# P V of a windowed attention in 128x64 tiles of two heads, with the values stored beside their zeros

## The chip, the cores and the metric

One core of one Trainium2 chip runs the whole program. The time is the device time of one execution in microseconds (us); the median of several executions counts. A profile is one further execution, taken by the hardware profiler. The engines are PE (TensorE, matmuls; PEld is its weight load), DVE (VectorE), ACT (ScalarE), POOL (GpSimd) and SP (SyncE, which here only issues DMAs and small waits). Each engine works through its own list of instructions in order, and waits at semaphores for the others.

## What is computed

The inputs are bf16: x of 2048 rows and 448 columns, the weights wqkv (448 x 1344) and wo (448 x 448) of an attention with 16 heads of 28 channels, and the weights w1 (448 x 1792) and w2 (1792 x 448) with biases b1, b2 of a feed-forward part. Each position attends to itself and to the positions 2, 4, ..., 14 before it.

```python
def _A_ref(x, wqkv, wo):
    H = 16; Dh = D // H
    W, dil = 8, 2
    q, k, v = ...
    idx = pos[:, None] - (jnp.arange(W) * dil)[None, :]
    logits = jnp.einsum("bhsd,bhswd->bhsw", q, kg) * Dh ** -0.5
    attn = _softmax(jnp.where(mask, logits, -1e9), axis=-1)
    o = jnp.einsum("bhsw,bhswd->bhsd", attn, vg)
    return o.reshape(B, S, D) @ wo
def _B_ref(x, w1, b1, w2, b2):
    return _gelu(x @ w1 + b1) @ w2 + b2
xn = _layernorm(A_x)
return A_x + _A_ref(xn, ...) * _silu(_B_ref(xn, ...))
```

## The kernel before

**Rows.** The rows are regrouped, even positions first and odd positions after, so that a window of 8 positions at distance 2 becomes 8 neighbours. There are 16 row tiles of 128 rows (`t`) and 4 chunks of 512 (`c`).

**Stages.** For each row tile: statistics (L434, L439), the normed x (L469) and its transpose into `xnT`, through PE for tiles 0 to 3 (L484) and by a transposing DMA on SP for the others (L389, `turn_x`). From `xnT` PE makes q and k (L569), copied to `qk_tok` (L328 on ACT, L330 on DVE) and transposed by DMA into `qkT`; and v (L592), copied to `v_tok`, stored in DRAM (`v_hbm`, L381, `store_v`) and read back from there in windows (`move_v`, also L381). The feed-forward part is L645 (with the gelu on ACT, L649) and L677; its gate is L717, L723, L727. The output projection with `wo` is L835, L843, then L850, L856 and the store L860.

**A visit of the attention.** There are 9 visits `b` of up to 228 positions, in 4 sub-blocks `s` of 57 (`NW`; visit 4 has 56). The keys of a sub-block are 64 neighbours, 57 and the 7 before them. `spread` copies the keys into `kd` (L629 on ACT, L631 on DVE) so that two heads stand side by side: keys of one head in columns 0 to 63, of the other in 64 to 127, each with the other head's channels multiplied by zero. The scores (L744, step "S") are 32 matmuls of a 64-row, 128-column tile over 57 streamed columns: 128 partitions of the result are 64 keys of one head and 64 of the other. ACT takes the exponential (L753) into `E`, four banks a visit, and DVE multiplies by a mask (L759). Then P V (L773, step "P"): for each of 4 sub-blocks, 4 channel groups `g`, 2 pairs `h` and 2 heads of a pair `a` one matmul that contracts the 64 keys of that head and gives 32 partitions, 28 channels and a sum of the weights that comes from a column of ones beside the values. That is 64 matmuls of a 64-row, 32-column tile; head `a` goes to bank `a`. For each of the two banks DVE transposes (L782), takes the reciprocal of the sums (L786), transposes back (L791) and multiplies into `oT` (L796).

**Values.** A `v_tok` row holds 2 x 8 x 32 elements, 28 channels and 4 ones per head. `move_v` reads for each head of the pair a window of 64 rows for 4 sub-blocks, 512 bytes a run, into partitions 0 to 63 or 64 to 127 of a ring `p_v` of 3 buffers.

**Order.** The program is planned before it is emitted: every step is a task with an engine, a cost in us, dependencies and a priority (the tables `PRIO`, `LATER` and `NUDGE`); the planner fills the engines, and the instructions are emitted in that order. Rings (`_Pool`) stand for buffers. Most row pairs run as two half pairs with a hop between them: a half-array matmul group, a no-op on POOL or SP that waits for it, and the other half. A P V takes a place in `p_f`, one place, given back 3.5 us (`BURST`) after the P V. `take` and `give` name what a task occupies. In the planner a P V costs 0.52 and a score step 0.48.

Of the kernel before, what the change touches and what calls it, by code (L numbers as in the profile page):

```python
# [8 lines left out]
F32 = mybir.dt.float32  # L9
BF16 = mybir.dt.bfloat16  # L10
# [7 lines left out]
TILED = 30  # L18
BURST = 3.5
NUDGE = {  # L20
    82: 164, 83: 221, 88: -17, 98: 114, 148: -76, 155: 52, 210: 248, 309: -202, 522: -191, 633: 96,
    635: 30, 656: -230, 898: 200, 985: 15,
}
LAST = 336
SAME = 20
HOPS = ("POOL", ("SP", "POOL"))
MASK_ON = ("DVE", 0.4)

# [147 lines left out]
def kernel(  # L176
# [51 lines left out]
    def sb(name, shape, dt=BF16):  # L228
        return const.tile(shape, dt, name=name)
# [24 lines left out]
    zero = sb("zero", [P, H * 32])  # L254
    mv = sb("mv", [P, NT, 2], F32)
    sd = sb("sd", [P, NT], F32)
    rstd = sb("rstd", [P, NT], F32)
# [6 lines left out]
    p_E = ring("E", 8, [P, 512], fifo=True)  # L264
    p_dt = ring("dt", 2, [P, 512], F32)
    p_rd = ring("rd", 2, [P, H], F32)
    p_y = ring("y", 2, [P, D], F32)
    p_t = ring("t", 2, [P, D], F32)
# [14 lines left out]
    PRIO = {  # L283
        "project": (213.5, 84.5, 145, 57.5,),
        "project2": (61, 74.5, 113.5, -640,),
        "values": (199.5, -20, 128, 6,),
        "attn": (784, 1451, 452, 363, 27.5, 240.5, 361.5, 160.5, 204.5,),
        "ff1": (198.5, 215, 158, 71.5, 146.5, 194, 121, 197.5, 124, 116, 171.5, 143, 137, 144.5,
            114.5, 194, 150.5, 78.5, -21, 12, 47, 112.5, 51.5, 61.5, 93.5, 59.5, 175, 137,),
        "gelu": (5, 143.5, 52.5, 123.5,),  # L290
        "ff2": (805.5, -34.5, 231, 114.5, -2.5, 89, -623.5, 135, 208.5, 180.5, -39.5, 104, -4, 131,
            -80.5, -689,),
        "final": (-141.5, 2, -11, -16.5, 187, -2, 125, 203, -49.5, 65.5, -59.5, 162.5, -51, 134,
            6.5, 220.5,),
        "norm": (131, 11, 219.5, 294, 190, 208.5, 173, -1.5, 189, 173.5, 166.5, 159, 150.5, -11.5,
            127, 56,),
        "loads": (2.5, 106.5, -29, 61, -61,),
        "stats": (49, 32, 205.5, 205.5, 55, 91.5, -4.5, 56, 70.5, 178.5, 31, 101.5, -704, 2.5, 161,
            70.5,),
        "turn_x": (198, 4.5, 200, 12.5, 20.5, 38.5, 81, 163, 190.5, 214.5, 8.5, -3, 72, 153.5,  # L300
            72.5, 162.5,),
        "turn_qk": (-12.5, 15, 13, 198, 91, 58, -98.5, 69, 181.5, 168, 69.5, -36, 142, 100, 88,
            80.5,),
        "move_v": (19.5, -58, -99, 107.5, 62, 44, 64.5, 3, 68,),
        "store_v": (55.5, 68.5, -38.5, -16, 175.5, 53, 3.5, 13.5, 115.5, -7, 113, 144.5, 69, 170.5,
            147.5, 61.5,),
        "spread": (120, 175.5, 70.5, 58.5, 20, 222, 105.5, 24, 126,),
        "copies": (187, 4, 219, 15.5, 90, 177, 88.5, 31, 29, 20.5, 182, 51, 204.5, 49.5, 24,),
    }
    LATER = {"swap": 102.5, "qk": -548.5, "v": 174.5, "gelu": 131.5, "exp": 44, "mask": -436, "pv": 158.5, "recip": 165.5, "os": 191, "y": 231, "tanh": -35.5, "g": 111.5, "sg": 40, "o": 208.5}  # L310

    plan = _Plan()

# [272 lines left out]
    def vproj(t, prio):  # L586
        k0 = t * P

        def part(ps, kt, half, start, stop):
            r = half_rows(half)  # L590
            w = w_in[r, kt, 2 * D:] if kt < 3 else w_in3[r, 1, :]
            return nc.tensor.matmul(ps[:, :D], xnT[r, kt, k0:k0 + P], w, start=start, stop=stop)  # L592

        def evac(a, own, i):
            v = v_tok[t % len(v_tok)]

            def fn(k):
                copy(k.on, v[:, :, :, :DH].rearrange("p a x c -> p x a c"),
                     buf(p_b, own, i)[:, :D].rearrange("p (x a c) -> p x a c", a=2, c=DH))
# [163 lines left out]
    def values_of(b, exps):  # L763
        n = VIS[b][1]

        def fn(banks):
            for s in range(4):
                for g in range(G):
                    for h in range(2):
                        for a in range(2):  # L770
                            r = slice(NK * a, NK * a + NK)
                            c0, c1 = (4 * h + s) * n, (G * (s % 2) + g) * n
                            nc.tensor.matmul(banks[a][32 * g:32 * g + 32, c0:c0 + n], buf(*v_at[b])[r, s, 2 * g + h, :],  # L773
                                             buf(p_E, exps[2 * h + s // 2])[r, c1:c1 + n], start=True, stop=True)
        return fn, tuple((p_E, e, 0) for e in exps) + (v_at[b],)

    def output_of(b, po, i, a, prio):
# [28 lines left out]
    def attn(b, what):  # L806

        prio = PRIO["attn"][b]
        if what == "S":
            fn, deps, give = scores_of(b)  # L810
            a = plan.add("PE", 0.48, lambda k: fn([buf(p_b, k, i) for i in range(4)]), deps + state["early"] + last_visit[what][-1:] + last_visit["P"][b - 2:b - 1],
                         prio, take=(p_b,) * 4, give=give, tail=0.15, mode=64)
# [5 lines left out]
        a = plan.add("PE", 0.52, lambda k: fn([buf(p_b, k, i) for i in range(2)]), masked + t_v[b] + last_visit[what][-1:],  # L818
                     prio + LATER["pv"], take=(p_b, p_b, p_f), give=give, tail=0.15, mode=33)
        plan.add("CLK", 0.0, None, [a], 300, give=((p_f, a, 0),), tail=BURST)  # L820
        last_visit[what].append(a)
# [199 lines left out]
```

## Time and profile before

| | us |
|---|---|
| median of 3 runs | 153.42 (153.25 to 153.74) |
| the profiled execution | 153.43 |
| its span | 151.7 |
| granted PE clock | 1.00 |
| DMA | 19.47 MB, 36983 packets |

The span runs from the first to the last instruction; the profiled execution has 1.73 us around it. In the lists of groups each row has the line, engine, operation, what is written and read, the shape and the count, then busy time, mean duration in ns of one, and idle time before them. On a time line each row has the start in us, the time from the first start to the last end, the engine, the line, and in brackets what ended an idle time before it. Matmuls overlap, so the busy time of a group is less than count times duration.

### The profile page before, as it was taken

The numbers are of one execution on the slowest core, as the hardware profiler recorded it, in microseconds if no ns is written. First come the engines' busy times: TensorE is split into PE (matmuls) and PEld (weight loads), VectorE is DVE, ScalarE is ACT, GpSimd is POOL, SyncE is SP. The second block draws the span as 40 slices with busy tenths as digits, with TensorE's granted clock in tenths as the row PEclk, the third lists the DMA queues.
The fourth block names the chain that finished last, engine by engine and source line by source line (L and its number), as shares of the span: only waits on it lengthen the run. The fifth ranks groups of instructions, "written<-read, shape, count | busy, mean of one in ns | idle before, by whom it ended". The sixth has DMA issues, their size and how long they took to land.

```text
span 151.7 us, 5225 instructions
## 1 busy us (share of the span) xinstructions
PE 146.6 (97%) x2169; PEld 79.7 (53%) x2169; DVE 118.7 (78%) x288; ACT 90.5 (60%) x160; POOL 24.9 (16%) x62
## 2 busy tenths in 40 slices
PE   7999999999999999999999999999999999999990
PEld 2457555555567555556555554445566444554560
DVE  3786850624996997799998998889898978997972
ACT  3234969368796959658444457967396497602030
POOL 7435540100046900231201000000000000000000
PEclk9999999999999999999999999999999999999999
DMA  5999985499987973699945516222020000001221
GB/s 158 315 297 318 175 233 123 41 172 338 250 187 194 212 188 77 133 185 210 184 131 130 140 57 133 78 73 62 12 65 6 0 0 4 4 0 61 90 68 31
DMA packets 36983, 19.47 MB, mean 128 GB/s; under 512 B 24840, under 2 KB 35919, under 8 KB 36959
## 3 DMA queue, kind: packets, MB, share of 16 engines
q1 hardware_dynamic: 35774, 16.40, 47.4%
q0 software_dynamic: 1040, 2.62, 6.9%
q8 instruction: 17, 0.28, 0.7%
q10 hardware_dynamic: 144, 0.11, 0.3%
q14 instruction: 8, 0.06, 0.1%
HBM read 9.42 MB, written 3.94 MB: 88 GB/s over the span
## 4 chain that ended last, share of the span: by engine, by line
PE 95%; DVE 2%; ACT 0%; issue 0%; DVEq 0%; ACTq 0%
PE bank L645 28%; PE bank L677 25%; PE bank L569 14%; PE bank L592 7%; PE bank L835 7%; PE bank L773 4%; PE bank L699 3%; PE bank L343 3%; PE bank L744 2%; PE bank L484 1%; DVE sg L850 1%; DVE w_in L727 1%; PE bank L843 0%; DVE qk_tok L330 0%; ACT t L723 0%
## 5 line engine op out<-in xcount | busy, mean ns | idle before, releaser
L645 PE MATMUL bank<-xnT,w 64*128 64x512 bf16 x392 | 44.3, 376 | 0.0
L677 PE MATMUL bank<-w,h 64*128 64x448 bf16 x392 | 40.4, 349 | 0.0
L649 ACT ACTIVATE h<-bank,b 128x512 bf16<-128x512 f32 x56 | 34.0, 688 | 9.7 <-PE bank L645 9.3
L645 PEld LDWEIGHTS <-w 64*128 64x128 bf16 x392 | 20.4, 94 | 20.4
L677 PEld LDWEIGHTS <-h 64*128 64x128 bf16 x392 | 19.2, 94 | 16.0
L569 PE MATMUL bank<-w_in,xnT 64*128 64x448 bf16 (+1 forms) x212 | 25.1, 349 | 0.1
L753 ACT ACTIVATE E<-bank 128x456 bf16<-128x456 f32 (+1 forms) x36 | 16.8, 557 | 9.3 <-PE bank L744 9.3
L328 ACT CAST qk_tok<-bank 128x448 bf16<-128x448 f32 x23 | 11.5, 540 | 9.9 <-PE bank L569 8.5
L723 ACT ACTIVATE t<-y 128x448 f32<-128x448 f32 x15 | 8.6, 586 | 14.5 <-DVE y L717 14.5
L569 PEld LDWEIGHTS <-xnT 64*128 64x128 bf16 (+1 forms) x212 | 11.7, 94 | 9.4 <-DVE xnT L330 0.3
L782 DVE STREAM_TRANSPOSE dt<-bank 128x480 f32<-128x480 f32 (+1 forms) x18 | 12.1, 674 | 2.8 <-PE bank L773 2.8
L592 PE MATMUL bank<-w_in,xnT 64*128 64x448 bf16 (+1 forms) x106 | 13.5, 349 | 0.1
L791 DVE STREAM_TRANSPOSE dt<-rd 128x480 f32<-128x480 f32 (+1 forms) x18 | 12.1, 675 | 0.6
L835 PE MATMUL bank<-wo,oT 64*128 64x448 bf16 x112 | 12.4, 349 | 0.0
L434 DVE BATCH_NORM_STATS2 st<-x_sb 128x6 f32<-128x448 bf16 x16 | 9.6, 604 | 3.3 <-DMA x_sb<-in_A_x_dram 3.3
L759 DVE TENSOR_TENSOR E<-E,m_gen 128x456 bf16<-128x456 bf16 (+1 forms) x32 | 11.1, 387 | 1.3 <-ACT E L753 1.3
L796 DVE TENSOR_TENSOR oT<-bank,dt 128x456 bf16<-128x456 f32 (+1 forms) x18 | 11.4, 631 | 0.6
L330 DVE CAST qk_tok<-bank 128x448 bf16<-128x448 f32 x9 | 5.4, 618 | 7.8 <-ACT h L649 5.5
L717 DVE TENSOR_TENSOR y<-bank,b 128x448 f32<-128x448 f32 x15 | 8.9, 618 | 1.6 <-PE bank L677 1.6
L381 POOL DMA_DIRECT2D v_hbm<-v_tok x11 | 6.3, 572 | 21.3 <-PE bank L592 10.0
L592 PEld LDWEIGHTS <-xnT 64*128 64x128 bf16 (+1 forms) x106 | 6.0, 94 | 4.5 <-issue 0.3
L835 PEld LDWEIGHTS <-oT 64*128 64x128 bf16 x112 | 5.5, 94 | 5.1
(72 smaller groups left out, 143.7 us busy)
## 6 DMA issues: line engine op xcount, KB each, us to landing
out_dram<-o SPq DMA_DIRECT2D x15, 112.0 KB, 1.7
v<-v_hbm SPq DMA_DIRECT2D x13, 128.0 KB, 3.2
v_hbm<-v_tok POOLq DMA_DIRECT2D x11, 128.0 KB, 3.6
w<-in_B_w_dram SPq DMA_DIRECT2D x2, 672.0 KB, 7.5
x_sb<-in_A_x_dram SPq DMA_DIRECT2D x3, 448.0 KB, 6.9
w_in<-in_A_wqkv_dram SPq DMA_DIRECT2D x3, 336.0 KB, 4.4
w<-in_B_w_dram SPq DMA_DIRECT2D x2, 448.0 KB, 5.3
w<-in_B_w_dram SPq DMA_DIRECT2D x2, 336.0 KB, 6.5
```

The costliest lines, as they stand in the source:

```text
L328: nc.scalar.copy(o, i)
L569: return nc.tensor.matmul(ps[:, :D], xnT[r, kt, cs], w, start=start, stop=stop)
L592: return nc.tensor.matmul(ps[:, :D], xnT[r, kt, k0:k0 + P], w, start=start, stop=stop)
L645: return nc.tensor.matmul(ps[:], w1[r, kt, ms], xnT[r, kt, cs], start=start, stop=stop)
L649: nc.scalar.activation(buf(p_h, own, i)[:], buf(p_b, own, i)[:], ACT.Gelu_apprx_tanh, bias=b1[:, mt:mt + 1])
L677: return nc.tensor.matmul(ps[:, :D], buf(*h_at[(c, mt)])[r, cs], w2[r, mt, :], start=start, stop=stop)
L753: nc.scalar.activation(buf(p_E, k)[:, :8 * n], buf(p_b, a, at + i)[:, :8 * n], ACT.Exp, scale=SCALE)
L759: nc.vector.tensor_tensor(out=E, in0=E, in1=m[:, :, :, :n].rearrange("p i g q -> p (i g) q"), op=ALU.mult)
L782: nc.vector.transpose(buf(p_dt, k)[:, :32 * m], buf(p_b, po, i)[:, :32 * m])
L791: nc.vector.transpose(buf(p_dt, d)[:, :32 * m].rearrange("p (b c) -> p b c", c=32), buf(p_rd, r)[:, :m].unsqueeze(2).to_broadcast((P, m, 32)))
L796: nc.vector.tensor_tensor(out=oT[:, a::2, q:q + 4 * n1], in0=buf(p_b, po, i)[:, :n].rearrange("p (l q) -> p l q", l=2), in1=buf(p_dt, d)[: ...
L835: return nc.tensor.matmul(ps[:, :D], oT[r, kt, t * P:(t + 1) * P], wo[r, kt, :], start=start, stop=stop)
```

## The change

The tile shape of P V. One matmul now contracts all 128 partitions of `E`, the 64 keys of both heads of a pair, and gives 64 partitions, 32 for each head. Its weights are a 128 x 64 block: the values of the first head in rows 0 to 63 and columns 0 to 31, those of the second in rows 64 to 127 and columns 32 to 63, and zeros elsewhere. There are 32 such matmuls a visit, and the channel group `g` decides bank and half (`i = g // 2`, `r = 64 * (g % 2)`). The loop over `h` is now the outer one.

The zeros are part of the stored values. `v_tok` is 2 x 8 x 64 elements; it is set to zero and then to one in the four columns beside each head. `v_hbm` has 1024 elements a row in place of 512, `p_v` doubles, and stores and moves carry 256 KB in place of 128 KB. The 7 rows ahead of the first position come from `wo`, which is zero at that time, in place of a buffer of zeros.

Because heads now lie in other partitions of the result, `wo` is loaded in 8 DMAs of 50 KB in place of 4 of 100 KB. `xnT` and `oT` are two views of one buffer `xT` of 3072 columns: `oT` columns 1024 to 2047 lie on `xnT` columns 0 to 1023. `p_E` and `p_dt` are cut to the width in use. `p_f` has three places, and the score steps take one too. The planner's costs are 0.44 and 0.41. The tables `PRIO`, `LATER` and `NUDGE` have new values throughout, so the order on every engine is a new one.

```diff
-    xnT = sb("xnT", [P, KT, S])
+    xT = sb("xT", [P, KT, HALF + S])
+    xnT, oT = xT[:, :, HALF:], xT[:, :, :S]
-    v_tok = [sb(f"v_tok{t}", [P, 2, H // 2, 32]) for t in range(4)]
-    v_hbm = dram.tile([BACK + S, H * 32], BF16, name="v_hbm")
-    oT = sb("oT", [P, KT, S])
+    v_tok = [sb(f"v_tok{t}", [P, 2, H // 2, 64]) for t in range(NV)]
+    v_hbm = dram.tile([BACK + S, H * 64], BF16, name="v_hbm")
...
-    p_v = ring("v", 3, [P, 4, H // 2, 32], fifo=True)
+    p_v = ring("v", 3, [P, 4, H // 2, 64], fifo=True)
-    p_f = _Pool([None])
+    p_f = _Pool([None] * 3)
...
-    t_vw = [plan.add("DVE", 0.08, memset("vector", v[:, :, :, DH:], 1.0), [t_on], prio=96) for v in v_tok]
+    t_vw = []
+    for v in v_tok:
+        t_vz = plan.add("DVE", 0.42, memset("vector", v[:], 0.0), [t_on], prio=94)
+        for a in range(2):
+            t_vz = plan.add("DVE", 0.07, memset("vector", v[:, a, :, 32 * a + DH:32 * a + 32], 1.0), [t_vz], prio=94)
+        t_vw.append(t_vz)
...
-                at = v_hbm[q:q + NK, a * H * 16:(a + 1) * H * 16]
-                return bass.AP(tensor=at.tensor, offset=at.offset, ap=[list(at.ap[0]), [n * H * 32, 4], [1, H * 16]])
+                at = v_hbm[q:q + NK, a * H * 32:(a + 1) * H * 32]
+                return bass.AP(tensor=at.tensor, offset=at.offset, ap=[list(at.ap[0]), [n * H * 64, 4], [1, H * 32]])
...
-            for s in range(4):
-                for g in range(G):
-                    for h in range(2):
-                        for a in range(2):
-                            r = slice(NK * a, NK * a + NK)
-                            c0, c1 = (4 * h + s) * n, (G * (s % 2) + g) * n
-                            nc.tensor.matmul(banks[a][32 * g:32 * g + 32, c0:c0 + n], buf(*v_at[b])[r, s, 2 * g + h, :],
-                                             buf(p_E, exps[2 * h + s // 2])[r, c1:c1 + n], start=True, stop=True)
+            for h in range(2):
+                for s in range(4):
+                    for g in range(G):
+                        i, r = g // 2, 64 * (g % 2)
+                        c0, c1 = (4 * h + s) * n, (G * (s % 2) + g) * n
+                        nc.tensor.matmul(banks[i][r:r + 64, c0:c0 + n], buf(*v_at[b])[:, s, 2 * g + h, :],
+                                         buf(p_E, exps[2 * h + s // 2])[:, c1:c1 + n], start=True, stop=True)
...
-    t_zero = plan.add("DVE", 0.27, memset("vector", zero[:], 0.0), [t_on], prio=90)
-    t_vpad = dma("SP", v_hbm[:BACK, :], zero[:BACK, :], 7, 70, [t_zero, t_x[TPC - 1]])
+    t_vpad = dma("SP", v_hbm[:BACK, :], wo[:BACK].rearrange("p l d -> p (l d)")[:, :H * 64], 14, 70, [t_wo[0], t_x[TPC - 1]])
...
-    t_wo += [dma("POOL", wo[32 * g:32 * g + 28, :, :], A_wo[112 * g:112 * g + 112, :].rearrange("(l c) d -> c l d", l=4),
-                 100, 80, [t_w2[1][0]] + t_wo[:1]) for g in range(G)]
+    for k in range(8):
+        gh, r = k // 4, k % 4
+        r0 = DH * (8 * gh + 4 * (r // 2) + r % 2)
+        src = A_wo[r0:r0 + 3 * DH, :].rearrange("(l c) d -> c l d", l=3)[:, 0:3:2, :]
+        t_wo.append(dma("POOL", wo[32 * r:32 * r + DH, gh::2, :], src, 50, 80, [t_w2[1][0]] + t_wo[:1]))
```

In the new order the four moves of visits 0 and 1 stand on SP (visit 0) behind the loads of x tiles 8 to 15 and on POOL (visit 1) behind the load of b2; the transposes of qk tiles 6, 4 and 5 follow the moves on SP, and the kd copies of visit 2 stand on DVE ahead of the last mask of visit 0. The output projection of row tiles 0 and 1 stands behind the P V of visits 1 and 2.

More of the change, by code (lines that the diff above doesn't have):

```diff
@@ L25 @@
 SAME = 20
+NV = 4
 HOPS = ("POOL", ("SP", "POOL"))
@@ L253 @@
     head = sb("head", [P, 2], F32)
-    zero = sb("zero", [P, H * 32])
     mv = sb("mv", [P, NT, 2], F32)
@@ L263 @@
     p_st = ring("st", 4, [P, 6], F32)
-    p_E = ring("E", 8, [P, 512], fifo=True)
-    p_dt = ring("dt", 2, [P, 512], F32)
+    p_E = ring("E", 8, [P, 8 * NW], fifo=True)
+    p_dt = ring("dt", 2, [P, 480], F32)
     p_rd = ring("rd", 2, [P, H], F32)
@@ new lines @@
+        "project": (199, 149.5, 133, -6.5,),
+        "project2": (-22, 7, 6, -1011,),
+        "values": (133, -902.5, 8, -172.5,),
+        "attn": (120.5, 128, 32, 142, 254.5, 234.5, -63, 107.5, 74,),
+        "ff1": (56, 18.5, 198, 41, 152.5, 23, 14, 69.5, 23.5, 85, 46.5, 13.5, 60, 105.5, -94.5, 14,
+            13.5, 209.5, 178.5, 107, 155.5, 19, 94.5, 45.5, 181.5, 78, 191, 15.5,),
+        "gelu": (200, 143.5, 52.5, 60,),
+        "ff2": (39, -34.5, 118, 114.5, 188, 89, -988.5, 135, -59.5, 180.5, -25.5, 104, 52.5, 131,
+            -5, -9.5,),
@@ new lines @@
+        "final": (107, 2, -13, -16.5, 169.5, -2, 39, 203, -907, 65.5, 141, 162.5, 150.5, 134, 29,
+            125,),
+        "norm": (131, 11, 219.5, 294, 99, 106.5, 54, 161.5, 155.5, 80.5, 185, 96, 6, 122.5, 199.5,
+            50.5,),
+        "loads": (-38.5, 192.5, -18, 68.5, -61,),
+        "stats": (49, 32, 205.5, 205.5, 184.5, 160, 100, 201.5, 5, 100.5, 216.5, 20, -18.5, 57,
+            101, 180,),
+        "turn_x": (198, 4.5, 200, 12.5, 33, 125.5, 99.5, 69.5, 71.5, 137.5, 157.5, 178.5, 116,
+            157.5, -75, 19,),
@@ L308 @@
+        "turn_qk": (46.5, -8, 155, 102.5, -74, -87.5, -13.5, -50, -13.5, 168, -6, 65.5, 148, 155,
+            44.5, 20,),
+        "move_v": (185.5, -654.5, 104, 36.5, 207, 157.5, -16.5, 109.5, 194,),
+        "store_v": (147, 19.5, 134, 15.5, 59.5, 170, 47.5, 92, 166.5, 124.5, -33, 100, 170.5, 202,
+            139, 11.5,),
+        "spread": (158.5, 82.5, 155, -33.5, 71.5, 119, 127.5, 33, 131.5,),
         "copies": (187, 4, 219, 15.5, 90, 177, 88.5, 31, 29, 20.5, 182, 51, 204.5, 49.5, 24,),
@@ L309 @@
     }
-    LATER = {"swap": 102.5, "qk": -548.5, "v": 174.5, "gelu": 131.5, "exp": 44, "mask": -436, "pv": 158.5, "recip": 165.5, "os": 191, "y": 231, "tanh": -35.5, "g": 111.5, "sg": 40, "o": 208.5}
+    LATER = {"swap": 946, "qk": -94.5, "v": -72, "gelu": 216, "exp": 306.5, "mask": -1022.5, "pv": 64.5, "recip": 158.5, "os": 200, "y": 473.5, "tanh": 117.5, "g": 132, "sg": 201.5, "o": 212}
     plan = _Plan()
@@ L597, in fn @@
             def fn(k):
-                copy(k.on, v[:, :, :, :DH].rearrange("p a x c -> p x a c"),
-                     buf(p_b, own, i)[:, :D].rearrange("p (x a c) -> p x a c", a=2, c=DH))
+                at = v[:, 0, :, :DH]
+                dst = bass.AP(tensor=at.tensor, offset=at.offset, ap=[list(at.ap[0]), list(at.ap[1]), [64 * (H // 2) + 32, 2], list(at.ap[2])])
+                copy(k.on, dst, buf(p_b, own, i)[:, :D].rearrange("p (x a c) -> p x a c", a=2, c=DH))
             t_vt[t] = plan.add(("ACT", "DVE"), (act(D), dve(D)), fn, [a, t_vw[t % len(v_tok)], t_vd.get(t - len(v_tok))], prio + LATER["v"], give=((p_b, own, i),))
@@ L810, in attn @@
             fn, deps, give = scores_of(b)
-            a = plan.add("PE", 0.48, lambda k: fn([buf(p_b, k, i) for i in range(4)]), deps + state["early"] + last_visit[what][-1:] + last_visit["P"][b - 2:b - 1],
-                         prio, take=(p_b,) * 4, give=give, tail=0.15, mode=64)
+            a = plan.add("PE", 0.44, lambda k: fn([buf(p_b, k, i) for i in range(4)]), deps + state["early"] + last_visit[what][-1:] + last_visit["P"][b - 2:b - 1],
+                         prio, take=(p_b,) * 4 + (p_f,), give=give, tail=0.15, mode=64)
+            plan.add("CLK", 0.0, None, [a], 300, give=((p_f, a, 0),), tail=BURST)
             last_visit[what].append(a)
@@ L817, in attn @@
         fn, give = values_of(b, exps)
-        a = plan.add("PE", 0.52, lambda k: fn([buf(p_b, k, i) for i in range(2)]), masked + t_v[b] + last_visit[what][-1:],
+        a = plan.add("PE", 0.41, lambda k: fn([buf(p_b, k, i) for i in range(2)]), masked + t_v[b] + last_visit[what][-1:],
                      prio + LATER["pv"], take=(p_b, p_b, p_f), give=give, tail=0.15, mode=33)
```

28 lines of the change are left out of this document (2 added, 26 removed).

## Prediction

> **What bounds the kernel now.** I read four views in this order: the page's engine lines and its chain of waits, the chain in order of time, the groups by form, and stretches of the time line. The page first: PE is busy 97% of the span, and the chain is PE for 95%.
>
> ```profile
> PE 146.6 (97%) x2169; PEld 79.7 (53%) x2169; DVE 118.7 (78%) x288; ACT 90.5 (60%) x160; POOL 24.9 (16%) x62
> PE 95%; DVE 2%; ACT 0%; issue 0%; DVEq 0%; ACTq 0%
> PE bank L645 28%; PE bank L677 25%; PE bank L569 14%; PE bank L592 7%; PE bank L835 7%; PE bank L773 4%; PE bank L699 3%; PE bank L343 3%; PE bank L744 2%; PE bank L484 1%; DVE sg L850 1%; DVE w_in L727 1%; PE bank L843 0%; DVE qk_tok L330 0%; ACT t L723 0%
> ```
>
> So a microsecond taken from PE between 6.5 us (first projection) and 147 us is a microsecond of the span, and every new wait of PE is one too. The chain in order of time has one step there that is not PE: a copy on DVE.
>
> ```profile
> 42.14 0.61 DVE qk_tok L330
> 42.76 0.04 issue
> 42.80 2.80 PE bank L592 x27
> ```
>
> One of 28 L592 matmuls had started before it, so PE stood still for about 0.3 us. Everything else is gapless. The P V step is small: line L773 is 9 visits of 64 matmuls, L744 (scores) 9 visits of 32.
>
> ```profile
> L773 PE MATMUL bank<-E,v 64*32 64x57 bf16 x512 | 5.6, 189 | 0.0
> L744 PE MATMUL bank<-qkT,kd 64*128 64x57 bf16 x256 | 5.0, 186 | 0.0
> ```
>
> A matmul lasts 186 to 189 ns but they overlap, so the price of a visit is read from starts on PE's time line.
>
> ```profile
> 63.02 0.70 PE L773 MATMUL bank<-E,v 64*32 64x57 bf16 x64
> 63.65 3.58 PE L569 MATMUL bank<-w_in,xnT 64*128 64x448 bf16 x36
> ...
> 68.39 0.62 PE L744 MATMUL bank<-qkT,kd 64*128 64x57 bf16 x32
> 68.84 0.73 PE L569 MATMUL bank<-w_in,xnT 64*128 64x448 bf16 x6
> ```
>
> The 64 P V matmuls start within 0.70 - 0.19 = 0.51 us, and the next tile shape starts 0.12 us after the last of them (0.63 in all). The 32 score matmuls start within 0.62 - 0.19 = 0.43 us, and the following group, of the same tile shape, starts at once (0.45 in all): 14 ns a matmul where two tiles of the array work side by side.
>
> **The change, part by part.** The sum is made against the profiled execution: 153.43 us, of which 151.7 is the span and 1.73 lies around it. The median of the runs is 153.42, so both stand alike.
>
> *P V on PE.* 64 matmuls of 64x32 become 32 of 128x64, two of which can lie side by side; the streamed width stays 57. No row shows this shape. Nearest is L744: also 32, also two at a time, 0.43 us; the shape changes before and after the visit, as now, so the 0.12 stays. 0.51 - 0.43 = 0.08 a visit, 9 visits: -0.75 us. Bounds: if half the count at the present 8 ns spacing were all, 0.26 us a visit, -2.3; if two column tiles did not overlap, 32 x 27 = 0.87 us a visit, +3.2. I take -0.75, by the row of the same count and width.
>
> The Trainium skill speaks against the change here: TensorEngine Tiling (Array Packing), section Restrictions, has column tiling switch off the fast weight load, and TensorE: Matmul & The Clock Gate, section LDWEIGHTS, gives a load one column per 1/1.2 ns. By these pages 64 columns are an estimated 53 ns, 16 loads in a row on each of two tiles 0.85 us, which would make a visit 0.34 us dearer and this term about +3.1 in place of -0.75; the L773 row, whose tiles are column tiles already, is no proof either way, as its 32-column loads are short enough to hide.
>
> *Start on DVE.* The four memsets of v_tok (128x64) become four of 512 words and eight short ones, and they stand before the first statistics; the zero memset goes.
>
> ```profile
> 0.94 0.33 DVE L335 MEMSET v_tok<- 128x64 bf16 x4
> 1.24 0.33 DVE L335 MEMSET qk_tok<- 128x64 uint32 x4
> ...
> 1.65 0.27 DVE L335 MEMSET zero<- 128x256 uint32 x1
> 3.35 0.63 DVE L434 BATCH_NORM_STATS2 st<-x_sb 128x6 f32<-128x448 bf16 x1 [1.43 <-DMA x_sb<-in_A_x_dram]
> ```
>
> 64 words take 112 ns and 256 take 272, so 512 take about 0.49. In the new order of DVE, seven of the short ones come ahead of the statistics; with a wait of a short one on its long one each v_tok costs some 0.6 us: qk_tok ends at 1.24, four times 0.6 makes 3.65. The statistics started at 3.35, when x landed. They start 0.3 later, and the chain to the first transposes and L569 has no slack: +0.3. Bounds 0 to +0.6.
>
> *Bytes.* Values go out and come back with their zeros: 16 stores and 18 moves of 128 KB become 256 KB. The quiet stretch 100 to 102 us holds two moves alone, 0.50 busy of all DMA engines over 2 us, so 0.5 us each; a doubled one costs 0.5 to 1.0. What counts is where they stand. On SP, three stores instead of one come ahead of the transposes of x tiles 4 to 7 (before 19.8 us), and four moves (two on SP, two on POOL, against one and one before) now stand behind the loads of x tiles 8 to 15, ahead of the transposes of qk tiles 4 to 7, in a stretch that is full:
>
> ```profile
> 29.00:37.00 8.00, 8.00 (x78) 4.21 (x76) 2.33 (x6) 5.39 (x10) 0.12 (x1) 1.00 1.02 229
> 37.00:43.00 6.00, 5.92 (x88) 3.34 (x86) 5.65 (x16) 5.03 (x10) 1.32 (x2) 1.00 1.19 264
> ```
>
> The last two columns are the busy share of the DMA engines and GB/s. Four moves add 2 to 4 us to it. Before, SP was through with those transposes at 44.6; it would be at 46 to 48, landing 2.5 to 4 later. In DVE's new order the kd copies of visit 2 wait for them ahead of the last mask of visit 0, which the first P V needs at about 51; and queued behind them on SP is the transpose of x tile 8, needed at 57, with about 1 us to spare where it had 7. That cover of 1 us is what is left; when it is gone PE waits. Bounds 0 to +3; I take +0.5, near the lower end, as the only such wait now shown is PEld's 0.4 us on a qkT transfer ahead of L773.
>
> *The new order.* The wait at 42 us goes (the copies that PE waits for come behind the statistics again, but PE has other banks in between): -0.3, bounds -0.3 to +0.3. A new one arises at the first output projection. From P V of visit 1 to the projection of row tiles 0 and 1, PE now has six half pairs (three of 0.57 and three of 0.76 us) and one P V (0.55), 4.5 us. DVE must in that time finish two y additions (released 1.1 us before that P V ends, 1.2 for the two) and two output chains, which the present order shows whole:
>
> ```profile
> 71.59 0.68 DVE L782 STREAM_TRANSPOSE dt<-bank 128x480 f32<-128x480 f32 x1 [0.15 <-PE bank L773]
> 72.31 0.25 DVE L786 RECIPROCAL rd<-dt 128x15 f32<-128x15 f32 x1
> 72.59 0.68 DVE L791 STREAM_TRANSPOSE dt<-rd 128x480 f32<-128x480 f32 x1
> ...
> 75.57 0.63 DVE L796 TENSOR_TENSOR oT<-bank,dt 128x456 bf16<-128x456 f32 x1
> ```
>
> 76.20 - 71.59 = 4.6 us; with 0.15 of y left over and 0.15 for the ways to DVE and back it is 4.9 against 4.5: +0.4 (0 to +1). Two more meetings come out with nothing to spare (P V of visit 6; the projection of tiles 10 and 11, which needs visit 6's second output 5.2 us after its P V): +0.15 together, 0 to +1.
>
> *At nothing.* wo arrives in 8 pieces, not 4: 2.4 us more of POOL's queue at 0.6 each, ahead of one hop that PE waits for with about 0.8 to spare. The zero rows from wo, oT in xnT's buffer (overwritten columns are those of tiles 0 to 7, read for the last time before 41 us) and three fewer copies on DVE lie beside PE. The tail, the 5.5 us from 146.2, where the chain leaves PE, to the end of the span, has the same instructions in the same order.
>
> Sum: -0.75 + 0.3 + 0.5 - 0.3 + 0.4 + 0.15 = +0.3: **153.7 us**, own range 153.0 to 154.5.
>
> **The rivals.**
> (1) *The order meets everything* (other side). All inputs of PE arrive in time, so only -0.75 + 0.3 - 0.3 count: 152.7. For it: the present order shows that such a schedule can keep PE gapless for 140 us. Against it: the 4.9 against 4.5. It decides if the output chains of visit 1 end within 4.5 us of its P V and no DMA is late. Chance 0.30.
> (2) *The doubled bytes bind.* The transposes land 3 us late, at 50 to 52 us, and PE waits at the first P V, at the third scores and at x tile 8: 1 to 2 us more than taken, 155.2 in the middle. For it: share 1.02 to 1.19 over 14 us. Against: larger pieces may cost no more than the old ones. 0.17.
> (3) *Column tiles take turns* (the rule above): +3.2 in place of -0.75, 157.7. 0.07.
> (4) *The shape brings nothing*: 32 starts in the old 0.51 us; +0.75, 154.5. Against it: L744. 0.08.
> The forecast has 0.38.
>
> **How the numbers follow.** A measurement of this kernel tells about 0.3% (0.46 us) from no change, so within means 152.96 to 153.88. Faster: (1), 0.30. Within: 0.17 of the forecast and 0.03 of (4), 0.20. Slower: 0.21 of the forecast, whose open terms (bytes, meetings) reach further up than down, 0.17, 0.07 and 0.05, 0.50. The range 152.4 to 155.5 leaves out (3), the upper part of (2) and what a visit near 0.26 us would gain, some 0.18.
>
> **What would show it.** P V: 32 starts in 0.43 us, 0.55 to the next shape. Start: first statistics at 3.65. Bytes: kd of visit 2 after 48 us, PE's wait for xT or kd near 51 or 57. Order: PE idle about 0.4 us ahead of the first output projection, none at 42. It is wrong if P V takes under 0.35 or over 0.6 us a visit, or if PE's idle time between 7 and 147 us is under 0.3 us.

## The result, and the profile after

The changed kernel takes 163.41 us (median of 4 runs, 162.59 to 163.66), beside 153.58 us (153.25 to 153.89) for the kernel before on the same chip: 1.063 times as long, 95% interval 1.059 to 1.068. The forecast was 153.7, the range 152.4 to 155.5. The profiled execution took 162.59 us, its span is 160.6 against 151.7: 8.9 us are to be found. (It was the shortest of the four, so the median holds about 0.8 us more that no trace shows.)

The page of the changed kernel, its engine line, the slices of PE, of its granted clock and of the DMA engines, and the chain:

```profile
PE 148.6 (93%) x1881; PEld 78.9 (49%) x1881; DVE 119.7 (75%) x292; ACT 91.3 (57%) x163; POOL 25.5 (16%) x63
...
PE   7999999999924999999999995999999999999990
...
PEclk9999999999996899999999999999999999999997
DMA  5999996699999998479977999980510001000121
...
PE 79%; DMA 11%; DVE 5%; ACT 2%; issue 1%; SPq 1%; POOLq 0%; DVEq 0%; ACTq 0%
```

The same slices of PE in the kernel before:

```profile
PE   7999999999999999999999999999999999999990
```

PE has two holes that it had not before, one in slices 12 and 13 (4 us each) and a small one in slice 25, and its clock falls behind the first. DMA, absent from the chain before, now holds 11% of it. Who PE waited for, us in total, times, longest:

```profile
PE bank L683 <- DMA w<-in_B_w_dram: 5.0, 1, 5.0
PE bank L574 <- POOLq L530: 1.9, 1, 1.9
PE bank L343 <- PEq L1013: 0.8, 1, 0.8
PE bank L489 <- DVE xn L474: 0.3, 1, 0.3
```

The first is the second ff matrix. The chain in order of time (start, us, what) shows how it came late:

```profile
37.81 1.85 ACT h L655 x3
39.67 0.22 SPq L394
...
39.93 0.59 SPq L376
...
40.56 9.68 DMA w<-in_B_w_dram
...
50.29 4.21 PE bank L683 x27
```

and SP's queue (start, us it held the queue) what was ahead of it:

```profile
30.54 2.58 SPq L386 DMA_DIRECT2D v<-v_hbm  x2
33.16 0.89 SPq L376 DMA_DIRECT2D w<-in_B_w_dram  x1
34.15 5.74 SPq L394 DMA_TRANSPOSE qkT<-qk_tok  x1
39.93 4.11 SPq L376 DMA_DIRECT2D w<-in_B_w_dram  x2
```

In the kernel before:

```profile
33.20 3.56 SPq L389 DMA_TRANSPOSE qkT<-qk_tok  x1
36.80 1.44 SPq L371 DMA_DIRECT2D w<-in_B_w_dram  x2
```

Two value moves of 256 KB on SP, two more on GpSimd at 31.8, then one transpose whose issue alone held SP for 5.74 us (3.56 before), so that the last two pieces of the matrix were issued at 40 us instead of 37, and landed 9.7 us later instead of 5.3. They came at 50.24; PE had run out of other work at 45.28.

The second hole, in the same chain: a store of values issued by SP at 90.46 lands at 97.70; the move of visit 6 waits for it on GpSimd, and behind that move stands the hop that PE's projection needs.

```profile
90.46 7.24 DMA v_hbm<-v_tok
...
97.72 0.04 POOLq L386
...
98.26 0.03 POOLq L530
...
98.33 0.74 PE bank L574 x6
```

Third, the granted clock (behind the stretch and its length comes PE's busy time; the last three columns are clock, DMA share, GB/s):

```profile
49.00:49.50 0.50, 0.00 (x0) 0.00 (x0) 0.00 (x0) 0.00 (x0) 0.00 (x0) 1.00 0.14 41
49.50:50.00 0.50, 0.00 (x0) 0.00 (x0) 0.00 (x0) 0.00 (x0) 0.00 (x0) 0.72 0.19 23
50.00:51.00 1.00, 0.71 (x4) 0.28 (x6) 0.00 (x0) 0.00 (x0) 0.00 (x0) 0.50 1.41 279
...
53.00:54.00 1.00, 1.00 (x14) 0.45 (x12) 0.39 (x1) 0.00 (x0) 0.00 (x0) 0.93 1.20 320
```

PE comes back at half clock: its first 28 L683 matmuls take 4.21 us from the end of the pause to the last one's end, where 28 in a gapless stretch move that end on by 2.65, so 1.55 us are lost. Fourth, the start on DVE:

```profile
1.33 2.86 DVE L335 MEMSET v_tok<- 128x512 uint32 x11
4.11 0.59 DVE L439 BATCH_NORM_STATS2 st<-x_sb 128x6 f32<-128x448 bf16 x1
```

First statistics at 4.11 instead of 3.35, first projection (L574, before L569) at 7.00 instead of 6.46: 0.54. Sum: 5.0 + 1.55 + 1.9 + 0.54 = 9.0, less the 0.3 that the kernel before lost at 42 us, 8.7 of 8.9. P V is not in the sum, for a visit takes what it took:

```profile
58.07 0.70 PE L778 MATMUL bank<-E,v 128*64 128x57 bf16 x32
58.70 1.50 PE L683 MATMUL bank<-w,h 64*128 64x448 bf16 x14
```

0.70 - 0.19 = 0.51 us for the starts, 0.63 to the next shape, to the hundredth the visit of 64 small matmuls before.

### The profile page after: what moved, and what is told of

Same layout as the page of the kernel before. It is cut to its first block, busy times and chain, and to the rows that moved or that the text cites. A ratio compares the mean times of both kernels' runs of the same rounds, so it can differ in the third digit from the quotient of the medians.

```text
span 160.6 us, 4663 instructions
## 1 busy us (share of the span) xinstructions
PE 148.6 (93%) x1881; PEld 78.9 (49%) x1881; DVE 119.7 (75%) x292; ACT 91.3 (57%) x163; POOL 25.5 (16%) x63
## 4 chain that ended last, share of the span: by engine, by line
PE 79%; DMA 11%; DVE 5%; ACT 2%; issue 1%; SPq 1%; POOLq 0%; DVEq 0%; ACTq 0%
PE bank L651 24%; PE bank L683 22%; PE bank L574 12%; PE bank L841 7%; DMA w<-in_B_w_dram 6%; PE bank L597 5%; DMA v_hbm<-v_tok 5%; PE bank L778 3%; PE bank L705 3%; PE bank L750 2%; DVE v_tok L335 2%; ACT h L655 1%; DVE sg L856 1%; DVE st L439 1%; PE bank L489 1%
## 5 line engine op out<-in xcount | busy, mean ns | idle before, releaser
L683 PE MATMUL bank<-w,h 64*128 64x448 bf16 x392 | 41.6, 358 | 5.0 <-DMA w<-in_B_w_dram 5.0
L651 PE MATMUL bank<-xT,w 64*128 64x512 bf16 x392 | 45.3, 376 | 0.0
L683 PEld LDWEIGHTS <-h 64*128 64x128 bf16 x392 | 19.1, 96 | 22.1 <-DMA w<-in_B_w_dram 5.5
L651 PEld LDWEIGHTS <-w 64*128 64x128 bf16 x392 | 19.0, 94 | 21.5
L574 PE MATMUL bank<-w_in,xT 64*128 64x448 bf16 (+1 forms) x212 | 26.5, 350 | 1.9 <-POOLq L530 1.9
L574 PEld LDWEIGHTS <-xT 64*128 64x128 bf16 (+1 forms) x212 | 11.8, 94 | 11.4 <-POOLq L530 2.3
L597 PE MATMUL bank<-w_in,xT 64*128 64x448 bf16 (+1 forms) x106 | 13.5, 349 | 0.0
L841 PE MATMUL bank<-wo,xT 64*128 64x448 bf16 x112 | 13.0, 349 | 0.0
L328 ACT CAST v_tok<-bank 128x448 bf16<-128x448 f32 x10 | 5.2, 534 | 13.5 <-PE bank L597 12.7
L801 DVE TENSOR_TENSOR xT<-bank,dt 128x456 bf16<-128x456 f32 (+1 forms) x18 | 11.4, 631 | 0.6
L637 DVE TENSOR_SCALAR kd<-qkT,head 128x1024 bf16<-128x1024 bf16 x13 | 5.8, 493 | 7.8 <-DMA qkT<-qk_tok 7.8
L841 PEld LDWEIGHTS <-xT 64*128 64x128 bf16 x112 | 5.7, 94 | 5.1 <-issue 0.4
```

The source lines that it names most:

```text
L328: nc.scalar.copy(o, i)
L574: return nc.tensor.matmul(ps[:, :D], xnT[r, kt, cs], w, start=start, stop=stop)
L651: return nc.tensor.matmul(ps[:], w1[r, kt, ms], xnT[r, kt, cs], start=start, stop=stop)
L683: return nc.tensor.matmul(ps[:, :D], buf(*h_at[(c, mt)])[r, cs], w2[r, mt, :], start=start, stop=stop)
L801: nc.vector.tensor_tensor(out=oT[:, a::2, q:q + 4 * n1], in0=buf(p_b, po, i)[:, :n].rearrange("p (l q) -> p l q", l=2), in1=buf(p_dt, d)[: ...
L841: return nc.tensor.matmul(ps[:, :D], oT[r, kt, t * P:(t + 1) * P], wo[r, kt, :], start=start, stop=stop)
```

## The experiments

Is it the body of the change or its new order? The tasks of both kernels correspond one to one, but for a few memsets, DMAs and clock marks, so that each body can be run with the other's order: the planner's choice is replaced by a table of (task, engine, start, end), each engine working off its tasks in that order. The same line serves for both.

```diff
+ORDER = [(task, engine, start, end),
...
+_Plan.run = _given
```

**Old body, new order.**

> The kernel before, with its 64x32 P V, its 128 KB stores and moves and its own buffers, but every engine works off its tasks in the order of the changed kernel. My reading of the two traces: the changed kernel loses 5.0 us at 45.3 us because four value moves of 256 KB went out ahead of the last pieces of the second ff matrix, 1.5 us more because PE ran at half clock for 3 us after that pause, 1.9 us at 96.4 us because a hop on GpSimd stands behind a value move that waits for a late store, and some 0.6 us at the start. Theory 'place and bytes together': with halved moves (4 x 0.75 us less of DMA time) the wait for the matrix shrinks to about 2 us, without a half clock, and the wait at 96 us stays: 156 to 158 us. Rival 'place alone': the wait stays near 5 us, 161 to 162. Rival 'bytes alone': both waits go, 153 to 154.

154.25 us (153.29 to 155.59, 10 runs) beside 153.72 (13 runs): ratio 1.0035, 0.9991 to 1.0079. This is near the rival "bytes alone" and below what my theory had. In the profiled execution, which at 155.6 was the longest of the ten, the wait for the matrix is 1.6 us, the half clock and the wait at 96 us are gone; the fastest runs are close to those of before.

**New body, old order.**

> The changed kernel's P V, zeros in the values, doubled stores and moves, wo in 8 pieces and shared buffer, but every engine works off its tasks in the order of the kernel before (the twelve memsets of the value buffers stand ahead of the first statistics, as in the changed kernel). Theory: P V costs the same (0.63 us a visit in both traces), the start is 0.6 us later, and the doubled bytes at the old places, where no value move stands ahead of the matrix, cost at most 1 us: 154 to 155.5 us. Rival 'bytes alone': the doubled bytes delay the matrix or the transposes wherever they stand: 157 or more. Rival 'P V is cheaper in a full schedule': under 153.5.

161.86 us (159.64 to 162.39), ratio 1.047, 1.037 to 1.058: my theory is refuted, the rival "bytes" holds. In the old order no value move stands ahead of the matrix, and PE waits elsewhere, for a transpose of x at 77.5:

```profile
PE bank L574 <- DMA xT<-xn: 5.0, 1, 5.0
```

The body costs 8 to 9 us in either order, the order 0.5 to 1.7 with either body. SP's queue just ahead of that wait, in the kernel before:

```profile
64.72 5.46 SPq L389 DMA_TRANSPOSE qkT<-qk_tok  x3
70.86 1.20 SPq L389 DMA_TRANSPOSE xnT<-xn  x1
```

and with the new body:

```profile
66.62 7.12 SPq L394 DMA_TRANSPOSE qkT<-qk_tok  x3
73.84 1.99 SPq L394 DMA_TRANSPOSE xT<-xn  x1
```

The transfers are the same ones; together they hold SP longer, the last is issued 3 us later and lands 8.6 us after that. And the pause brings half clock, here twice as long:

```profile
81.00:82.00 1.00, 0.00 (x0) 0.00 (x0) 0.00 (x0) 0.00 (x0) 0.00 (x0) 0.68 0.95 90
82.00:83.00 1.00, 0.48 (x4) 0.26 (x6) 0.00 (x0) 0.00 (x0) 0.00 (x0) 0.50 1.24 310
...
88.00:89.00 1.00, 1.00 (x12) 0.52 (x10) 1.00 (x2) 0.97 (x2) 0.00 (x0) 0.91 0.00 0
```

5.0 of pause, 2.8 (half of the 5.7 us that PE ran at half clock) and 0.8 at the start (first projection at 7.24 instead of 6.46) are 8.6, of 8.7 to be found (8.4 between the spans, and the 0.3 at 42 us, which this run does not lose).

**The two places in the changed kernel, one at a time.** Tasks are taken out of the planned order and put behind another one, nothing else differs.

```diff
+MOVES = (((217, 218, 219, 220), 305), ((221, 222, 223, 224), 348))   # e_moves: visits 0 and 1
+MOVES = (((517, 518, 519, 520), 945),)                               # e_hop: visit 6
```

> The changed kernel with one thing put elsewhere: the value moves of visits 0 and 1 (two on SP, two on GpSimd) are issued behind the last two pieces of the second ff matrix (SP) and behind the second pair of rstd steps (GpSimd) instead of ahead of the matrix. Theory: the 5.0 us wait at 45.3 us and the half clock behind it go, the wait at 96 us and the start stay: 156 to 157.5 us, clock 1.00. Rival: the queue of DMA engines is full there whatever the order (transposes of qk take it), so the matrix is still late: 160 or more. Rival: the wait passes on to the first P V, whose values now come later: 159 to 161.

157.49 us (157.27 to 157.58): 5.9 less than the changed kernel, as the theory said (6.5). The wait for the matrix and the half clock behind it are gone; left are 1.8 at the hop, and new ones of 1.0 (a transpose of x, at 31 us) and 0.3 (a hop behind the pieces of wo, near 56).

> The changed kernel with one thing put elsewhere: the value move of visit 6 (first half on GpSimd, second on SP) is issued behind the three hops of GpSimd that stood behind it. Theory: PE no longer waits 1.9 us at 96.4 us, all else stays: 161 to 161.8 us. Rival: that time was slack of something else that is late at the same place (the store of the values, the transposes of the last qk tiles), so the wait only changes its name: 163 to 164.

161.31 us, but 158.94 to 163.83. The wait at 96 us is gone in the trace; the wait for the matrix, which this kernel kept, was 3.1 us in the profiled run instead of 5.0, and that spread hides what the one place is worth in time: the median lies in my range, but the runs show neither the theory nor the rival.

**Is it the form of P V?**

```diff
+                        for a in range(2):
+                            q, o = slice(64 * a, 64 * a + 64), r + 32 * a
-                        nc.tensor.matmul(banks[i][r:r + 64, c0:c0 + n], buf(*v_at[b])[:, s, 2 * g + h, :],
+                            nc.tensor.matmul(banks[i][o:o + 32, c0:c0 + n], buf(*v_at[b])[q, s, 2 * g + h, 32 * a:32 * a + 32],
```

> The changed kernel, but P V reads the stored values in 64x32 tiles again (64 matmuls a visit, each the 32 columns of one head that are not zero), with the same order and the same doubled transfers. Theory: the form of P V is worth nothing either way (0.63 us a visit): within 0.8 us of the changed kernel, 162 to 164 us on a chip with the same before. Rival: the 128x64 tiles gain 0.08 us a visit as I forecast: 0.75 us above the changed kernel, with 0.7 us a visit in the trace.

164.62 us (163.31 to 166.3, 4 runs): 1.069 times before (1.065 to 1.072), the changed kernel 1.063 (1.059 to 1.068). The old form, fed from the doubled values, waits at the same places (5.0 at the matrix, 2.4 at the hop). The traced run is the longest of the four: the half clock behind the matrix lasts twice as long as in the changed kernel, and the 2.4 us at the hop brings another one:

```profile
100.00:101.00 1.00, 0.28 (x4) 0.19 (x6) 0.12 (x1) 0.00 (x0) 0.34 (x1) 0.96 1.18 345
101.00:102.00 1.00, 1.00 (x8) 0.37 (x6) 1.00 (x3) 0.10 (x1) 0.30 (x1) 0.50 0.61 147
```

A visit:

```profile
59.98 0.68 PE L780 MATMUL bank<-E,v 64*32 64x57 bf16 x64
60.59 2.82 PE L683 MATMUL bank<-w,h 64*128 64x448 bf16 x28
```

0.61 us to the next shape against 0.63: over nine visits the old form is 0.2 us cheaper, if anything. The medians lie 1.2 us apart the other way (0.8 without the longest run), more than my theory had and by themselves what the rival had; but the ranges overlap, the waits and the half clock in these runs spread by more than that, and the rows exclude that the new form gains 0.08 a visit.

Do its two column tiles overlap at all? All 16 matmuls of one, then all 16 of the other:

```diff
-            for h in range(2):
-                for s in range(4):
-                    for g in range(G):
-                        i, r = g // 2, 64 * (g % 2)
+            for r in (0, 64):
+                for h, s, i in [(h, s, i) for h in range(2) for s in range(4) for i in range(2)]:
```

> The changed kernel, with the 32 matmuls of a visit of P V in another order: all 16 of the first column tile, then all 16 of the second, instead of one by one in turn. It is looked at for the length of a visit only. Theory: the 0.51 us in which 32 matmuls start is two column tiles working side by side, 32 ns a matmul on each; without a neighbour each costs at least its 57 columns and its load, 0.85 to 1.1 us a visit. Rival: the two tiles never overlapped, 16 ns is one matmul's own time: still 0.51 us.

```profile
L778 PE MATMUL bank<-E,v 128*64 128x57 bf16 x256 | 8.8, 195 | 0.0
```

8.8 us for 8 visits, 1.10 each, 0.91 for the starts: 29 ns a matmul without a neighbour, 16 with one. They do overlap. In its single run, 162.89 us, PE waited 3.4 us for the matrix and 1.0 at the hop, and no half clock followed; that is 4 us less than in the changed kernel and covers the 3.6 that the visits cost more.

**The new form without the bytes.** Zeros written once on the chip, values stored and moved as 128 KB; the columns of a tile then lie at a stride of 8 elements.

```diff
-    p_v = ring("v", 3, [P, 4, H // 2, 64], fifo=True)
+    p_v = ring("v", 3, [P, 4, 2, 32, H // 2], fifo=True)
-buf(*v_at[b])[:, s, 2 * g + h, :],
+buf(*v_at[b])[:, s, :, :, 2 * g + h].rearrange("p a c -> p (a c)"),
```

> The changed kernel with P V in the same 128x64 tiles and every engine in the same order, but the zeros are not copied any more: they are written once into the three buffers of the values on the chip (six memsets of 64 partitions on DVE near 23 us), and values are stored and moved as blocks of 32 columns by 8 pairs of heads, 128 KB as before the change, so that a tile's 64 columns lie at a stride of 8 elements. The memsets ahead of the first statistics are short again. Theory: what costs is the 25 us of DMA time that the doubled transfers add; without it the wait for the matrix shrinks to 0 to 1.6 us, the one at 96 us goes, P V stays at 0.63 us a visit: 153.3 to 154.8 us. Rival 'the order': over 157. Rival 'the strided weights load slower': a visit of P V over 0.8 us, and 155 to 156.

> As the one with compact values, and the value moves of visits 0, 1 and 6 stand where the two earlier experiments put them (behind the second ff matrix, behind the hops). Theory: nothing of the pause ahead of the second ff matrix is left, nor the 0.3 us that the kernel before loses at 42 us: 152.6 to 153.4 us. Rival: another transfer is late in its place (the transposes of x tiles 8 to 15): 154 or more.

176.46 and 176.40 us: failures, for reasons of their own. Copies into the strided values and weights read at that stride:

```profile
L328 ACT CAST v_tok<-bank 128x448 bf16<-128x448 f32 x10 | 21.2, 2269 | 5.0 <-PE bank L599 4.1 <-ACT qk_tok L328 0.8
```
```profile
L778 PEld LDWEIGHTS <-v 128*64 128x64 bf16 x288 | 18.0, 215 | 3.6 <-issue 3.6
```

2269 ns a copy instead of 534, a weights load of 215 ns instead of 112, a visit of 2.04 us. PE's waits in the first of them are nearly all on those copies and none on a DMA, which agrees with the bytes as cause, but the times prove nothing about it.

**The bytes alone.** The kernel before, its own order and P V; each store writes its values twice, each move brings both halves.

```diff
-lambda: v[:].rearrange("p a x c -> p (a x c)"), [t_vt[t]]
+lambda: v[:].rearrange("p a x c -> p (a x c)").unsqueeze(1).to_broadcast((P, 2, H * 32)), [t_vt[t]]
-                at = v_hbm[q:q + NK, a * H * 16:(a + 1) * H * 16]
+                at = v_hbm[q:q + NK, :H * 32]
```

> The kernel before with its order and its P V; only the bytes are doubled: each store writes its 128 KB of values twice (256 KB), each move brings the rows of both halves of the heads (256 KB), of which P V reads the half that it read. (For room on the chip the attention output lies in the buffer of the normed x, as in the change.) Theory 'bytes': PE waits some 5 us for transposes of x tiles 8 to 15 near 77 us, with a half clock behind it, as the changed body did in this order: 159 to 162 us. Rival 'the rest of the body' (zeros in tiles, wo in 8 pieces, memsets at the start): 153.5 to 155.5.

158.91 us (157.69 to 164.19; 1.032, 1.027 to 1.037). Bytes alone cost 5.4 us by the median, just under the 159 that the theory began at; the rival "the rest of the body" is refuted. The trace, of the shortest run, shows 3.5 of them: 2.1 on a transpose of x at 78.6 us, where the changed body paused in this order, 0.6 on another at 26.5, and 0.8 at 71.5 on masks, held on DVE by kd copies that waited for a late transpose of qk. These pauses bring no half clock; another run, of 159.02 us, had a mean clock of 0.983, where the kernel before on this chip never had less than 0.993. Then by halves, 18 moves or 16 stores:

> As the one with doubled bytes, but only the 18 moves are doubled, the 16 stores are 128 KB again. Theory: the transfers have a limited amount of slack (some 16 us of DMA time between 6 and 96 us by the shares before, against 25 us added); 13 us more just fits: 153.5 to 156 us. Rival 'each byte costs': about half of the way from before to the doubled one, 156.5 to 158.

> As the one with doubled bytes, but only the 16 stores are doubled, the moves are 128 KB. Theory: 12 us more of DMA time just fits: 153.5 to 156 us. Rival 'each byte costs': 156.5 to 158.

153.63 us (ratio 1.0003, 0.9983 to 1.0024) and 157.37 us (1.027, 1.023 to 1.031). The stores cost 3.8 us by the median of four runs from 155.10 to 158.26, as the rival had it; the trace is of the shortest, 1.6 us above before, and waits 1.4 us for a transpose of x. The moves alone cost nothing, though they raise the DMA share between 6 and 96 us more (0.82 before, 0.99 with moves, 0.96 with stores). SP's queue with doubled moves, then with doubled stores:

```profile
64.79 5.57 SPq L389 DMA_TRANSPOSE qkT<-qk_tok  x3
70.92 1.20 SPq L389 DMA_TRANSPOSE xT<-xn  x1
```
```profile
64.94 8.11 SPq L389 DMA_TRANSPOSE qkT<-qk_tok  x3
73.14 2.04 SPq L389 DMA_TRANSPOSE xT<-xn  x1
```

Taken alone, only the stores delay the transposes that matter. Four of them are issued at 63 to 66 us, right beside these. To tell a store's own price from its place, only those four were doubled, then only the other twelve:

```diff
+            if t in (8, 9, 10, 11):
```

> The kernel before with its order; only the stores of row tiles 8 to 11 (the four that GpSimd issues at 63 to 66 us) are doubled. Theory 'place': these four delay the transposes behind them, so PE waits 1 to 2 us for x near 77 us again: 155 to 157.5 us. Rival 'each store costs': a quarter of the 3.8 us that all sixteen cost, 154.5.

> The kernel before with its order; all stores but those of row tiles 8 to 11 are doubled. Theory 'place': no transfer that PE waits for stands close behind them: 153.4 to 154.2 us. Rival 'each store costs': three quarters of the 3.8 us, 156.4.

154.52 us (1.0085, 1.006 to 1.011) and 153.60 us (1.0023, 0.9989 to 1.0057). The first alone falls on the rival's number, a quarter of 3.8, and under the 155 that my theory began at; the second refutes the rival, which had 156.4. SP's queue at the three transposes, with the four stores doubled, then with the twelve:

```profile
64.81 7.79 SPq L389 DMA_TRANSPOSE qkT<-qk_tok  x3
```
```profile
64.72 5.54 SPq L389 DMA_TRANSPOSE qkT<-qk_tok  x3
```

So a store costs by its place: four at the wrong one 1.0 us, less than I had given them, twelve elsewhere nothing that can be told. But 1.0 and 0.1 do not make the 3.8 of all sixteen, nor 3.8 and 0 the 5.4 of everything: by the medians the twelve, and the moves, cost only together with the four. How they do so was not taken apart.

**Everything mended at once,** and the old body in a mended new order:

```diff
+MOVES = (((217, 218, 219, 220), 305), ((221, 222, 223, 224), 329), ((517, 518, 519, 520), 945), ((62, 63, 64), 140), ((65, 66, 67), 158))
```

> The changed kernel with all its parts; the value moves of visit 0 stand behind the second ff matrix, those of visit 1 behind wo, that of visit 6 behind the hops, and the memsets of the third and fourth value buffer behind the first normed tiles. Theory: of the changed kernel's loss nothing but small rests is left, since P V costs the same in both forms: 153.3 to 155 us. Rival: doubled transfers that are taken from one place are late at the next: over 156.

159.01 us (157.14 to 161.95; 1.027, 1.022 to 1.031): the rival holds, for the shorter two runs too (157.14 and 158.23). The waits for the matrix and at the hop are gone from the trace, and PE waits for other transfers: transposes of x, 2.6 and 1.1 us, and 2.0 behind DVE and ACT, which a late transpose of qk had held up; one of the memsets, at 11.4 us ahead of a copy of qk, is in the chain itself. It is no better than taking the moves of visits 0 and 1 away alone (157.49).

> The kernel before with all its own parts in the order of the changed kernel, and the value moves of visits 0, 1 and 6 put behind the second ff matrix and behind the hops. Theory: the 1.6 us wait that this order showed goes: 152.6 to 153.4 us, the same as with compact values in 128x64 tiles, since both forms of P V take 0.63 us a visit. Rival '128x64 tiles are the cheaper form after all': 0.5 us or more above the one with compact values.

153.36 us (153.15 to 153.52) beside 153.63: ratio 0.9981, 0.9966 to 0.9995. Here PE has no gap between 7 and 147 us, the 0.3 us at 42 us included. It has the lowest median here, 0.2% under the kernel before, less than I said a measurement tells. The comparison with the compact values that this text announces fell through with them.

## Why the prediction was wrong, step by step

*Bytes, +0.5 (0 to +3): the step that failed.* In the trace of the changed kernel it measured some 8.4 us: 5.0 of wait for the matrix, 1.55 of half clock behind it, 1.9 at the hop. The bytes alone, in the old order, cost 5.4. Three things were wrong in it. The price: I let a doubled transfer cost 0.5 to 1.0 us of all DMA engines where one cost 0.5, so at most 0.5 more. By the queues' shares on the two pages, (0.558 + 0.113) x 160.6 = 107.8 us against (0.474 + 0.069) x 151.7 = 82.4, the 34 transfers took 25.4 us more, 0.75 each (an estimate: transfers that share the engines hold them longer, and shares above 1 occur, so part of it is crowding). The count: I counted the four moves and three stores near the place I looked at, of 34. The share between 6 and 96 us was 0.82, so about 16 us were free there; with everything doubled it was 1.04, 20 us more, and a sum over all transfers would have warned of that. It would not have given the price: 15 us more of moves alone (0.99) cost nothing, 13 of stores (0.96) cost 3.8. And who is late: I named kd of visit 2 (after 48 us; it ran at 53.6) and x tile 8, and overlooked that the last pieces of the second ff matrix stand in the same queue behind the same moves, with less cover than either. Taking the moves away from there gave 5.9 us back.

The rival "the doubled bytes bind" (0.17) had the mechanism, transposes that land late; its 155.2 was mis-sized by the same three points, had PE wait at other places and lacked the half clock.

*Half clock: not in the prediction.* 1.55 us here, 2.8 with the new body in the old order. A wait of 2.4 us or more can have a second price; the last section says when it did.

*P V, -0.75: wrong, nothing was gained.* The row I took it from, L744, has two tiles of rows; two tiles of columns start a matmul every 16 ns, not 14, and 32 x 16 ns is what 64 x 8 was. The rival "the shape brings nothing" was right and had 0.08. The rule of the Trainium skill (TensorEngine Tiling (Array Packing), Restrictions) did not bite: with its loads at 112 ns apiece, overlapping, the visit is as long as before, not 0.34 us longer, and even one column tile after the other starts a matmul every 29 ns.

*Start, +0.3 (0 to +0.6):* right in kind, 0.54; a v_tok costs 0.74 us (0.50 and two short ones of 0.12 together, with a wait ahead of each), not 0.6, and four stand ahead of the statistics at 4.11.

*New order:* the 0.3 us at 42 us went, as said. The 0.4 ahead of the first output projection and the two meetings of 0.15 did not come: PE works through from 54 to 96 us. That alone would prove little, as the pause gave the other engines time to get ahead; but the old body in the mended new order has no pause, and no gap there either. What came was the 1.9 us at the hop: a move that waits on GpSimd for a late store holds every hop behind it. I had asked who is queued behind a wait for SP, and not for GpSimd there. With the old bytes in the same order that wait does not exist, so it too is put down to the bytes at that place.

*At nothing:* the shared buffer and the tail cost nothing (the chain leaves PE 5.3 us ahead of the end, 5.5 before). The eight pieces of wo cost nothing in the changed kernel, and 0.3 us once, when the moves stood ahead of them.

What stays open: the new body in the old order (161.9) against the bytes alone (158.9) differ by 3 us; pause, half clock and start account for 8.6 of 8.7 us in the trace of the first, the pauses for 3.5 of 4.3 in that of the second, but why the pause at the transpose of x is 5.0 in the one and 2.1 in the other was not tried by itself.

## What to carry to other kernels

A transfer that is hidden is still paid for from what the DMA engines have free: when bytes grow, sum the growth over all transfers and hold it against the free share of the whole stretch. That sum only warns (here 15 us of moves went in free and 13 us of stores did not), so look in each issuing queue for the tightest thing behind the grown transfers, whatever it carries, and give any PE pause of more than 2 us a chance of a second price. And price a new tile shape by a row of the same kind of tiling; the same count and width are not enough.

## What the hardware showed unasked

The granted clock falls to half and stays there for one or two spells of 3.4 us. Worked out from the windows (clock 0.72 over half a us is 0.28 us at half), it was low from 49.72 to 53.14 in the changed kernel, 3.42 us, and from 81.36 to 88.18 with the new body in the old order, 6.82, twice that. The length of a pause does not tell whether it falls: 2.4 us did it in the run with the old form of P V and 3.1 in the one with the hop moved, while 2.6 with everything mended and 3.4 with the column tiles in turn did not. What the traces show in its place: in the 3.4 us just before each fall in mid-kernel PE had stood still for 2.4 (old form, at the hop), 2.8 (hop moved) or all 3.4 us (the other falls). The two falls in the run with the old form, at 49.72 and 100.92, lie 51.20 us apart, 15 spells of 3.413. By such steps, counted back from the clock's fall in the tail of their own traces (159.75 and 159.60), the pause of 3.4 that brought none is split by an edge into 1.8 and 1.5, and of the 2.6 at most 1.8 fall into one step. The second spell followed where PE was still idle for 1.0 us (old form, behind the matrix) or 1.2 (new body, old order) of the first; with 0.6 (changed kernel) and 0.3 (hop moved) of idle there was none. The Trainium skill (TensorE: Matmul & The Clock Gate, Part 1) has a free-running window of 3413 ns after which an idle PE is throttled and a busy one released; the lengths agree with it, and so does that the place of the window decides. But PE need not be idle for the whole window: here 2.4 us of it were enough, and 1.8 were not.

An ACT copy of 448 columns that writes with steps of 16 bytes took 2269 ns instead of 534, a DVE one 2191, and weights read at a stride of 8 elements load in 215 ns instead of 112 and make a visit three times as long.

The same three DMA transposes held SP for 5.5 us in the kernel before, 7.1 with the new body, 7.8 with the four stores beside them doubled and 8.1 with all stores doubled. So other transfers delay not only those in flight but all that SP has not issued yet.
